# VectorE's 16-bit passes of far tiles are ordered behind GpSimd's norm steps in a conformer layer

## The chip, the cores and the metric

The kernel runs on 1 core of one Trainium2 chip. The metric is the device time of one execution in microseconds (us), the median of several runs. Five engines work side by side, each through its own queue in program order: PE (TensorE, matrix products), ACT (ScalarE, activation functions), DVE (VectorE, elementwise work), POOL (GpSimd) and SP (SyncE, which only issues DMAs here).

## The reference

Two sequences (B = 2) of T = 4000 tokens with D = 144 channels pass through one conformer layer; all tensors are bfloat16.

```python
h = _layernorm(x);  x = x + 0.5 * (_silu(h @ w_ff1a) @ w_ff1b)          # 144 -> 576 -> 144
h = _layernorm(x);  qkv = h @ w_qkv                                     # H = 4 heads of 36
p = _softmax(einsum('bhqd,bhkd->bhqk', q, k) * Dh ** -0.5)              # 4000 x 4000 per head
x = x + einsum('bhqk,bhkd->bhqd', p, v) @ w_o
h = _layernorm(x);  a, b = split(h @ w_pw1);  h = a * _sigmoid(b)
c = depthwise convolution of h over 5 tokens;  x = x + _silu(c) @ w_pw2
h = _layernorm(x);  x = x + 0.5 * (_silu(h @ w_ff2a) @ w_ff2b)
return _layernorm(x)
```

There are five layer norms per token, and 2 x 4 x 4000 x 4000 exponentials.

## The kernel before

Tokens are worked on in 16 chunks of up to 512 (8 per sequence). All of X stays in on-chip memory. The attention runs over 32 groups (a chunk of queries and a pair of heads), each over 31 tiles of 128 keys, with the last 32 keys apart (`rest`).

**A plan written by a scheduler.** The program has no fixed order. `Rec.op` (L55) records each instruction with its tiles and a cost in us, and keeps a clock of its own: `free[eng]` is the time at which an engine is done by the plan, `o.done` the time at which others may use the result. `Sched` holds the stages of all chunks as threads (Python generators). A thread asks for an engine with `need(eng, slots, kids, cond, rank)`; `slots` is something that has a time from which it is available (`best`). `start_of` works out when a thread could go on, `best` takes, among those within 0.05 us of the earliest, the one with the smallest rank, and `advance` lets it record its next instructions. When all is recorded, `finish` works out from the data dependences which semaphores each instruction must wait for, and `replay` writes each engine's queue in the recorded order. So every instruction has one line in the profile, L146. Costs decide the order; on the chip only data dependences hold anything back.

**Exponentials.** For most tiles PE writes scores to PS and ACT makes PT = exp(PS) of both heads of the pair at once (128 x 1024), `emit_exp`. To relieve ACT, DVE does some tiles by bit arithmetic. For a *far tile* (`far_tiles`, taken from the end of a group's list of tiles) DVE moves each head's scores into the 16-bit buffer PU (a `tensor_scalar` from PS, 128 x 512, cost 0.07 + 512/960). In a *split tile* DVE does so for one head and ACT does the other; two such halves share a PU buffer. There are NPD = 2 buffers of PU, PF and PC. `exact` (L965) then corrects the result in four passes over 128 x 1024 16-bit values, all from and to on-chip memory SBUF: PF <- PU (bitwise and, cost 0.335), PC <- PF (0.335), PC <- PC x PF (two inputs, 0.6), PU <- PU + PC (two inputs, 0.6). Then PE multiplies PU with VA, and the buffer is free. The passes have rank RELAX = 1, after everything else that could start at the same time, or HURRY = -2 where the group is nearly done.

**Norms.** `ln` works on half a chunk: DVE takes statistics (`bn_stats`, ST <- X), POOL makes 1/sqrt(var + eps) from them in two steps on 128 x 2 values (RS <- ST, cost 0.22; power, RS <- RS,NHALF, cost 0.71), and DVE applies it (XN, two instructions). Statistics and both POOL steps are recorded in one step of the thread. The result is turned by SP's transposing DMAs (by PE at the start and the end) and used by the next matrix product. POOL does nothing else in the main part but copies of convolution edges between chunks (UA <- UA, UB <- UB, in `post1`), for which the convolution on PE waits.

Of the kernel before, what the change touches and what calls it, by code (L numbers as in the profile page):

```python
# [28 lines left out]
LERP_B = 127.0 * 128.0 + 0.128  # L29
QUAD_C = 130.0  # L30
QUAD_K = 0.333 / 128.0


class Op:
# [3 lines left out]
class Rec:  # L38
# [8 lines left out]
    def __init__(self, nc):  # L47
        self.nc = nc
        self.ops = []
        self.n = {}  # L50
        self.hist = {}
        self.free = {e: 1.0 for e in self.ENGS}
        self.kind = None
        self.last = 0.0

    def op(self, eng, name, *a, r=(), w=(), q=None, cost=0.1, kind=None, lat=None, **k):
        o = Op()
        o.eng, o.name, o.a, o.k, o.q = eng, name, a, k, q
        o.deps, o.inc, o.cnt = [], False, 0
        lane = eng if q is None else "q:" + q  # L60
        o.idx = self.n.get(lane, 0)
        self.n[lane] = o.idx + 1
        for key in r:
            h = self.hist.setdefault(key, ([], []))
            o.deps += [(d, True) for d in h[0]]
            h[1].append(o)
        for key in w:
            h = self.hist.setdefault(key, ([], []))
            o.deps += [(d, False) for d in h[0] + h[1] if d is not o]
            if h[1] and not (len(h[1]) == 1 and h[1][0] is o):  # L70
                self.hist[key] = ([o], [])
            else:
                h[0].append(o)
        start = self.free[eng]
        for d, raw in o.deps:
            if d.eng != eng or d.q is not None or (raw and eng != "pe"):
                start = max(start, d.done - self.NEAR.get((d.eng, eng), 0.0))
        if eng == "pe":
            if kind != self.kind:
                start += 0.1  # L80
            self.kind = kind
        self.free[eng] = start + cost
        o.done = start + cost + (self.LAT[eng] if lat is None else lat) + (0.045 if kind == "q" else 0.0)
        self.last = o.done
        self.ops.append(o)
        return o

# [69 lines left out]
class Slots:  # L157
# [12 lines left out]
    def best(self):  # L170
        return min(self.free.values())

    def take(self):
        i = min(self.free, key=lambda j: (self.free[j], j))
        del self.free[i]
        self.held.add(i)
        return i
# [4 lines left out]
            self.free[i] = self.R.last  # L182


class Thread:
    def __init__(self, gen, ready):
        self.gen, self.ready, self.live = gen, ready, True
# [3 lines left out]
def need(eng, slots=None, kids=(), cond=None, rank=None):  # L191
    return (eng, slots, kids, cond, rank)
# [6 lines left out]
class Sched:  # L199
# [26 lines left out]
        return kids  # L226

    def advance(self, th, item):
        self.cur = th
        n0 = len(self.R.ops)  # L230
        self.stepped = False
        try:
            th.req = th.gen.send(item)
        except StopIteration:
            th.live = False
            self.threads.remove(th)
        new = self.R.ops[n0:]
        if new:
            th.ready = max(th.ready, max(o.done for o in new))
# [29 lines left out]
def bass_standalone__conformer_family_zipformer__speech_kernel(  # L269
# [27 lines left out]
    R = Rec(nc)  # L297
    op = R.op
    S = Sched(R)

    def sb(name, shape, dt=BF16):
        return nc.alloc_sbuf_tensor(name, [128] + list(shape), dt)
# [28 lines left out]
    PU = sb("PU", [NPD, 2, CH], U16)  # L331
    PF = sb("PF", [NPD, 2, CH], U16)
    PC = sb("PC", [NPD, 2, CH])
# [38 lines left out]
    def load(eng, q, dst, src, w, r=()):  # L372
        op(eng, "dma_start", dst, src, q=q, w=w, r=r, cost=0.7)
# [9 lines left out]
    def load_ff(eng, q, WA, WB, wa, wb, nm):  # L383
        load_k(eng, q, WA, wa, [(nm, "a", 0)], [nm + "0"])
        load(eng, q, WB[:, 0:4, :], wb[0:512, :].rearrange("(t p) d -> p t d", p=128), [(nm, "b", 0)])
        for j in range(2):
            load(eng, q, WB[64 * j:64 * j + 64, 4 + j, :], wb[512:FF, :], [(nm, "b", 1 + j)])

    op("dve", "memset", WA1[0:HD, 1, :], 0.0, w=["W10"], cost=0.7)
    op("dve", "memset", WQKV[0:HD, 1, :], 0.0, w=["WQKV0"], cost=0.5)  # L390
    op("pool", "memset", XN[:, :, :, D:DP], 0.0, w=["XNP"], cost=2.0)
    for W, nm in ((WO, "WO0"), (WP1, "WP10"), (WA2, "W20")):
# [37 lines left out]
    for i in range(NWARM):  # L430
        op("pe", "matmul", PSV[:, i % 8, 0:256], lhsT=DUM[:, 0:128], rhs=DUM[:, :], start=True, stop=True,
           r=["DUM"], w=[("ps", i % 8)], cost=0.15)
# [522 lines left out]
    def late(more=0):  # L955
# [3 lines left out]
            return True  # L959
        return o_grp[0] // 2 - len(post_done) > (LAG if g < 20 else LAG_END) + more  # L960

    pair = [None]
    split = {}

    def exact(u, n, gi):  # L965


        def rank():
            return HURRY if s_grp[0] > gi or len(left[gi]) <= NEAR_END else RELAX

        yield need("dve", rank=rank)
        op("dve", "tensor_scalar", PF[:, u, :, 0:n], PU[:, u, :, 0:n], 127, None, op0=ALU.bitwise_and,
           r=[("PU", u)], w=[("PF", u)], cost=0.335)
        yield need("dve", rank=rank)
        op("dve", "tensor_scalar", PC[:, u, :, 0:n], PF[:, u, :, 0:n], QUAD_C, QUAD_K, op0=ALU.subtract, op1=ALU.mult,
           r=[("PF", u)], w=[("PC", u)], cost=0.335)
        yield need("dve", rank=rank)
        op("dve", "tensor_tensor", PC[:, u, :, 0:n], PC[:, u, :, 0:n], PF[:, u, :, 0:n], op=ALU.mult,
           r=[("PC", u), ("PF", u)], w=[("PC", u)], cost=0.6)
        yield need("dve", rank=rank)  # L980
        op("dve", "tensor_tensor", PU[:, u, :, 0:n], PU[:, u, :, 0:n], PC[:, u, :, 0:n], op=ALU.add,
           r=[("PC", u), ("PU", u)], w=[("PU", u)], cost=0.6)

    def bits_outputs(gi, u, kts, done):

        b, qc, p = groups[gi]
        n = width(gi)
        yield from exact(u, n, gi)
        yield need("pe", cond=lambda: o_grp[0] == gi and begun_group(gi))
        outputs(gi, [[] if kt is None else [(VA[:, b, kt, 2 * p + hh, :], PU[:, u, hh, :].bitcast(BF16))]  # L990
                     for hh, kt in enumerate(kts)],
                [("PU", u), "VA1"] + [("VA", b * CPB + c) for c in sorted({kt // NB for kt in kts if kt is not None})])
        pdp.give(u)
        output_done(gi, done)
# [51 lines left out]
    def next_tile():  # L1046

        g = s_grp[0]
        while g < len(groups) and not left[g]:
            g += 1  # L1050
        return (g, left[g][0]) if g < len(groups) else None

    def s_start():

        gi, kt = next_tile()
        b, qc, p = groups[gi]
        kc = b * CPB + kt // NB
        if kc not in kv_done or b * CPB + qc not in kv_done:
            return None
        t = max(R.free["pe"], R.ready(("WKT", kc)), R.ready(("WQT", (b * CPB + qc) % NQS)))  # L1060
        return max(t, exps[len(tiles) - 2]) if len(tiles) >= 2 else t
# [81 lines left out]
    while len(ff1_done) < CPB or 0 not in kv_done:  # L1143
        t, th = S.best()
        S.run(th)
    banks.restrict([6, 7])
    while banks.held - banks.only:
        t, th = S.best()
        S.run(th)

    for r in range(4):
        op("pe", "matmul", PSV[:, 4 + r // 2, r % 2 * 256:r % 2 * 256 + 256], lhsT=DUM[:, 0:128], rhs=DUM[:, :],
           start=True, stop=True, skip_group_check=True, r=["DUM"], w=[("ps", 4 + r // 2)], cost=0.107, kind="f")
# [20 lines left out]
    while next_tile() is not None or n_e < len(tiles):  # L1174
        a = s_start() if next_tile() is not None else R.free["pe"]
# [4 lines left out]
        t, th = S.best()  # L1180
# [23 lines left out]
    while o_grp[0] < len(groups):  # L1204
        emit_pending(force=True)
        if o_grp[0] < len(groups):
            t, th = S.best()
# [7 lines left out]
    while S.threads:  # L1215
        t, th = S.best()
# [34 lines left out]
```

## Time and profile before

| | |
|---|---|
| median of 3 runs | 986.31 us (985.67 to 987.59) |
| the profiled execution | 988.83 us, its span 987.0 us |
| ACT: exponentials PT <- PS | 808.9 us in 883 instructions |
| DVE: evictions PU <- PS | 189.8 us in 284 instructions |
| DVE: the four kinds of pass | 58.8 + 58.8 + 96.0 + 96.1 us, 143 of each |
| POOL: norm steps | 40.7 + 115.3 us, 160 of each |

The span is from the first to the last instruction of the core. A group's line gives the engine, the operation, the tiles written and read, shapes, the count, busy time and mean ns, and after the last bar the idle time of the engine ahead of such instructions with what ended it. A line of the timeline gives start, duration, engine, operation, tiles, and in brackets the engine's idle time before it and what released it. Matrix products are pipelined and their ends modelled. On DVE and ACT the shown durations of neighbours overlap a little, so what an instruction takes of the engine is read from start to start.

### The profile page before, as it was taken

The numbers are of one execution on the slowest core, as the hardware profiler recorded it, in microseconds if no ns is written. First come the engines' busy times: TensorE is split into PE (matmuls) and PEld (weight loads), VectorE is DVE, ScalarE is ACT, GpSimd is POOL, SyncE is SP. The second block draws the span as 40 slices with busy tenths as digits, with TensorE's granted clock in tenths as the row PEclk, the third lists the DMA queues.
The fourth block names the chain that finished last, engine by engine and source line by source line (L and its number), as shares of the span: only waits on it lengthen the run. The fifth ranks groups of instructions, "written<-read, shape, count | busy, mean of one in ns | idle before, by whom it ended". The sixth has DMA issues, their size and how long they took to land.

```text
span 987.0 us, 25520 instructions
## 1 busy us (share of the span) xinstructions
PE 893.5 (91%) x10852; PEld 344.3 (35%) x10852; DVE 846.0 (86%) x1903; ACT 908.4 (92%) x1168; POOL 168.8 (17%) x395
## 2 busy tenths in 40 slices
PE   8999898999898999999999998998889888898989
PEld 6733233232232323333343333333223232233358
DVE  7767999989988999988898999887898988887874
ACT  5798999999998999999999999998999999989952
POOL 6420020101013120211112020201111111101112
PEclk9999999999999999999999999999999999999999
DMA  4000020101011020111100010110001010101000
GB/s 135 2 1 2 12 43 13 33 2 39 18 29 33 13 44 9 22 28 24 23 8 12 12 35 12 29 13 17 18 13 29 13 29 12 29 2 25 16 18 13
DMA packets 73281, 21.67 MB, mean 22 GB/s; under 512 B 70592, under 2 KB 73168, under 8 KB 73168
## 3 DMA queue, kind: packets, MB, share of 16 engines
q1 hardware_dynamic: 72128, 19.58, 10.1%
q8 instruction: 85, 1.39, 0.6%
q10 hardware_dynamic: 1040, 0.48, 0.2%
q14 instruction: 28, 0.23, 0.1%
HBM read 3.31 MB, written 2.30 MB: 6 GB/s over the span
## 4 chain that ended last, share of the span: by engine, by line
PE 40%; ACT 36%; DVE 19%; POOL 3%; issue 2%; DMA 0%; SPq 0%; ACTq 0%
PE PS L146 40%; ACT PT L146 30%; DVE PU L146 6%; ACT TH L146 4%; DVE PC L146 3%; POOL RS L146 2%; DVE XN L146 2%; DVE OTF L146 1%; DVE HT L146 1%; DVE ST L146 1%; DVE X L146 1%; DVE PF L146 1%; ACT HT L146 1%; ACT PR L146 0%; DVE CB L146 0%
## 5 line engine op out<-in xcount | busy, mean ns | idle before, releaser
L146 ACT ACTIVATE PT<-PS 128x1024 bf16<-128x1024 f32 (+2 forms) x883 | 808.9, 1008 | 22.9 <-PE PS L146 20.3
L146 PE MATMUL PS<-QT,KT 64*64 64x512 bf16 (+2 forms) x4032 | 417.9, 391 | 58.1 <-ACT PT L146 44.9
L146 PE MATMUL PS<-PT,VA 64*37 64x512 bf16 (+1 forms) x3400 | 340.3, 374 | 2.5 <-DVE OTF L146 1.5
L146 PEld LDWEIGHTS PS<-QT,KT 64*64 64x64 bf16 (+1 forms) x4032 | 122.6, 103 | 322.4 <-ACT PT L146 193.3
L146 DVE TENSOR_SCALAR PU<-PS 128x512 uint16<-128x512 f32 (+1 forms) x284 | 189.8, 674 | 26.1 <-PE PS L146 23.2
L146 POOL TENSOR_SCALAR RS<-ST 128x2 f32<-128x2 f32 (+1 forms) x160 | 40.7, 254 | 707.9 <-DVE ST L146 707.3
L146 POOL TENSOR_TENSOR RS<-RS,NHALF 128x2 f32<-128x2 f32 (+1 forms) x160 | 115.3, 720 | 13.4
L146 PEld LDWEIGHTS PS<-PT,VA 64*37 64x37 bf16 x3400 | 98.5, 96 | 18.4 <-DVE OTF L146 2.5
L146 DVE TENSOR_SCALAR XN<-X,ST,RS 128x144 bf16<-128x144 bf16 (+1 forms) x310 | 82.6, 313 | 17.5 <-POOL RS L146 16.7
L146 DVE TENSOR_TENSOR PC<-PC,PF 128x1024 bf16<-128x1024 bf16 (+1 forms) x143 | 96.0, 675 | 1.6
L146 DVE TENSOR_TENSOR PU<-PU,PC 128x1024 uint16<-128x1024 uint16 (+1 forms) x143 | 96.1, 673 | 1.2
L146 ACT ACTIVATE TH<-PS 128x512 bf16<-128x512 f32 (+2 forms) x140 | 84.5, 604 | 5.2 <-PE PS L146 4.2
L146 PE MATMUL PS<-XT,WA 72*128 72x512 bf16 (+3 forms) x256 | 71.8, 379 | 7.0 <-DVE PU L146 2.9
L146 DVE SCALAR_TENSOR_TENSOR X<-PS,X 128x288 bf16<-128x288 f32 (+1 forms) x128 | 56.6, 453 | 23.1 <-PE PS L146 22.0
L146 DVE SCALAR_TENSOR_TENSOR HT<-TH,PS 128x512 bf16<-128x512 bf16 (+2 forms) x110 | 67.7, 620 | 5.5 <-ACT TH L146 5.2
L146 DVE BATCH_NORM_STATS2 ST<-X 128x6 f32<-128x288 bf16 (+1 forms) x160 | 69.0, 451 | 0.7
L146 PE MATMUL PS<-PU,VA 64*37 64x512 bf16 (+1 forms) x568 | 55.9, 378 | 9.2 <-DVE PU L146 8.4
L146 DVE TENSOR_SCALAR PC<-PF 128x1024 bf16<-128x1024 uint16 (+1 forms) x143 | 58.8, 414 | 1.6
L146 DVE TENSOR_SCALAR PF<-PU 128x1024 uint16<-128x1024 uint16 (+1 forms) x143 | 58.8, 416 | 1.1
L146 PE MATMUL PS<-WB,HT 128*128 128x144 bf16 (+1 forms) x640 | 56.4, 228 | 2.1 <-DVE HT L146 1.2
L146 PEld LDWEIGHTS PS<-WB,HT 128*128 128x128 bf16 (+1 forms) x640 | 39.9, 101 | 36.1 <-issue 22.3
L146 DVE TENSOR_REDUCE OTF<-PS 128x512 f32<-128x1024 f32 (+1 forms) x32 | 38.4, 1200 | 16.1 <-PE PS L146 15.2
(97 smaller groups left out, 623.2 us busy)
## 6 DMA issues: line engine op xcount, KB each, us to landing
X<-in_x_dram SPq DMA_DIRECT2D x14, 144.0 KB, 3.7
out_dram<-XN SPq DMA_DIRECT2D x28, 72.0 KB, 1.8
XT<-XN SPq DMA_TRANSPOSE x82, 2.5
XT<-AN SPq DMA_TRANSPOSE x28, 2.5
X<-in_x_dram SPq DMA_DIRECT2D x2, 117.0 KB
out_dram<-XN SPq DMA_DIRECT2D x4, 58.5 KB
WA<-in_w_ff1a_dram ACTq DMA_DIRECT2D x1, 144.0 KB, 2.9
WB<-in_w_ff1b_dram ACTq DMA_DIRECT2D x1, 144.0 KB, 3.5
```

Of the source, the lines that this page charges most:

```text
L146: ins = getattr(eng, o.name)(*o.a, **o.k)
```

## The change

The plan's clock learns about two things. (1) An instruction marked `port=True`, which are the four passes of `exact`, is taken to hold off GpSimd: a POOL instruction that would end by the plan before the last such pass has ended is put at that pass's end + 0.13; and if a pass starts while the last POOL instruction is running by the plan and ends after it, that instruction's end, and the time at which its thread goes on, move to the pass's end + 0.13. (2) Each pass asks for a `Quiet` slot, available from POOL's planned end less SLACK = 0.6 us; until then the scheduler gives DVE to other threads, or plans a hole. No instruction gets a wait; the arithmetic is unchanged.

```diff
+SLACK = 0.6
...
-    def op(self, eng, name, *a, r=(), w=(), q=None, cost=0.1, kind=None, lat=None, **k):
+        self.run_end = 0.0
+        self.behind = None
+        self.cur = None
+
+    def op(self, eng, name, *a, r=(), w=(), q=None, cost=0.1, kind=None, lat=None, port=False, **k):
...
-        self.free[eng] = start + cost
-        o.done = start + cost + (self.LAT[eng] if lat is None else lat) + (0.045 if kind == "q" else 0.0)
+        end = start + cost
+        if eng == "pool" and self.run_end > end - 0.05:
+            end = self.run_end + 0.13
+        if port:
+            self.run_end = end
+            if self.behind is not None and start < self.free["pool"] - 0.05 < end:
+                p, th = self.behind
+                late = end + 0.13 - self.free["pool"]
+                self.free["pool"] += late
+                p.done += late
+                if th is not None:
+                    th.ready = max(th.ready, p.done)
+        self.free[eng] = end
+        o.done = end + (self.LAT[eng] if lat is None else lat) + (0.045 if kind == "q" else 0.0)
         self.last = o.done
+        if eng == "pool":
+            self.behind = (o, self.cur)
...
+class Quiet:
+    free = True
+
+    def __init__(self, R):
+        self.R = R
+
+    def best(self):
+        return self.R.free["pool"] - SLACK
+
+    def take(self):
+        return None
...
-        self.cur = th
+        self.cur = self.R.cur = th
...
+    quiet = Quiet(R)
...
-        yield need("dve", rank=rank)
+        yield need("dve", quiet, rank=rank)
         op("dve", "tensor_scalar", PF[:, u, :, 0:n], PU[:, u, :, 0:n], 127, None, op0=ALU.bitwise_and,
-           r=[("PU", u)], w=[("PF", u)], cost=0.335)
+           r=[("PU", u)], w=[("PF", u)], cost=0.335, port=True)
```

The other three passes of `exact` are changed in the same two places.

More of the change, by code (lines that the diff above doesn't have):

```diff
@@ L969, in rank @@
             return HURRY if s_grp[0] > gi or len(left[gi]) <= NEAR_END else RELAX
-        yield need("dve", rank=rank)
+        yield need("dve", quiet, rank=rank)
         op("dve", "tensor_scalar", PF[:, u, :, 0:n], PU[:, u, :, 0:n], 127, None, op0=ALU.bitwise_and,
-           r=[("PU", u)], w=[("PF", u)], cost=0.335)
-        yield need("dve", rank=rank)
+           r=[("PU", u)], w=[("PF", u)], cost=0.335, port=True)
+        yield need("dve", quiet, rank=rank)
         op("dve", "tensor_scalar", PC[:, u, :, 0:n], PF[:, u, :, 0:n], QUAD_C, QUAD_K, op0=ALU.subtract, op1=ALU.mult,
-           r=[("PF", u)], w=[("PC", u)], cost=0.335)
-        yield need("dve", rank=rank)
+           r=[("PF", u)], w=[("PC", u)], cost=0.335, port=True)
+        yield need("dve", quiet, rank=rank)
         op("dve", "tensor_tensor", PC[:, u, :, 0:n], PC[:, u, :, 0:n], PF[:, u, :, 0:n], op=ALU.mult,
-           r=[("PC", u), ("PF", u)], w=[("PC", u)], cost=0.6)
-        yield need("dve", rank=rank)
+           r=[("PC", u), ("PF", u)], w=[("PC", u)], cost=0.6, port=True)
+        yield need("dve", quiet, rank=rank)
         op("dve", "tensor_tensor", PU[:, u, :, 0:n], PU[:, u, :, 0:n], PC[:, u, :, 0:n], op=ALU.add,
-           r=[("PC", u), ("PU", u)], w=[("PU", u)], cost=0.6)
+           r=[("PC", u), ("PU", u)], w=[("PU", u)], cost=0.6, port=True)
     def bits_outputs(gi, u, kts, done):
```

## The prediction

> **What bounds the kernel now.** I read the page first: the busy shares, the chain that ended last, the costliest groups.
>
> ```profile
> span 987.0 us, 25520 instructions
> PE 893.5 (91%) x10852; PEld 344.3 (35%) x10852; DVE 846.0 (86%) x1903; ACT 908.4 (92%) x1168; POOL 168.8 (17%) x395
> PE 40%; ACT 36%; DVE 19%; POOL 3%; issue 2%; DMA 0%; SPq 0%; ACTq 0%
> L146 ACT ACTIVATE PT<-PS 128x1024 bf16<-128x1024 f32 (+2 forms) x883 | 808.9, 1008 | 22.9 <-PE PS L146 20.3
> L146 POOL TENSOR_SCALAR RS<-ST 128x2 f32<-128x2 f32 (+1 forms) x160 | 40.7, 254 | 707.9 <-DVE ST L146 707.3
> L146 POOL TENSOR_TENSOR RS<-RS,NHALF 128x2 f32<-128x2 f32 (+1 forms) x160 | 115.3, 720 | 13.4
> L146 DVE TENSOR_TENSOR PC<-PC,PF 128x1024 bf16<-128x1024 bf16 (+1 forms) x143 | 96.0, 675 | 1.6
> ```
>
> PE and ACT share the end; DVE and POOL matter where they make those two late. ACT spends 808.9 of its 908.4 us on the attention exponentials. An order is better if it leaves ACT fewer gaps or moves more exponentials to DVE.
>
> Then the part in which far tiles run, in the windows view: 62 to 945 us as a whole, and of the eight 100 us stretches from 100 to 900 the first, the emptiest and the last.
>
> ```profile
> 62.00:945.00 883.00, 797.66 (x9747) 275.13 (x9744) 775.33 (x1681) 849.75 (x1061) 126.36 (x290) 0.99 0.11 20
> 100.00:200.00 100.00, 89.12 (x1104) 29.80 (x1104) 95.30 (x201) 98.41 (x119) 11.78 (x28) 1.00 0.14 25
> 300.00:400.00 100.00, 90.06 (x1050) 30.43 (x1050) 89.80 (x197) 93.60 (x117) 19.51 (x43) 0.98 0.15 27
> 800.00:900.00 100.00, 86.35 (x1065) 28.19 (x1068) 88.16 (x183) 94.73 (x115) 13.90 (x30) 0.98 0.10 18
> ```
>
> The columns are PE, weight loads, DVE, ACT, POOL. ACT is busy 849.75 of 883 us, so it idles 33; DVE idles 108. Between stretches ACT's idle time goes from 1.6 to 6.4 us, a standard deviation of about 1.6.
>
> Then GpSimd's two norm steps by tile (shortest, middle, longest ns), and, from the waits of 62 to 945 us, who waits for them and what ACT waits for.
>
> ```profile
> L146 POOL TENSOR_SCALAR RS<-ST x160: 188/193/1492, 5.6 to 981.6; 128x2 f32<-128x2 f32 x140, 104x2 f32<-104x2 f32 x20
> L146 POOL TENSOR_TENSOR RS<-RS,NHALF x160: 690/690/1138, 5.9 to 981.9; 128x2 f32<-128x2 f32 x140, 104x2 f32<-104x2 f32 x20
> ```
>
> ```profile
> DVE XN L146 <- POOL RS L146: 8.8, 13, 1.1
> ```
>
> ```profile
> ACT PT L146 <- PE PS L146: 20.3, 45, 3.1
> ```
>
> So most norm steps run unhindered, and a few are held off, one to 1.49 us. Against 160 steps at the middle duration the surplus is 40.7 − 160 × 0.193 = 9.8 us and 115.3 − 160 × 0.69 = 4.9 us. That is the whole resource that the change is about: some 15 us on an engine with 17% load. What counts is how much of it reaches ACT.
>
> Last, the timeline at the two kinds of place where it does. First a copy of convolution edges on GpSimd:
>
> ```profile
> 310.54 0.69 DVE L146 TENSOR_TENSOR PC<-PC,PF 128x1024 bf16<-128x1024 bf16 x1
> 310.69 2.13 POOL L146 COPY UA<-UA 128x2 bf16<-128x2 bf16 x1 [1.85 <-DVE UA L146]
> 311.14 0.43 DVE L146 TENSOR_SCALAR PC<-PF 128x1024 bf16<-128x1024 uint16 x1
> 311.48 0.69 DVE L146 TENSOR_TENSOR PU<-PU,PC 128x1024 uint16<-128x1024 uint16 x1
> 312.08 0.69 DVE L146 TENSOR_TENSOR PC<-PC,PF 128x1024 bf16<-128x1024 bf16 x1
> ...
> 313.00 1.04 PE L146 MATMUL PS<-UA,DG 128*128 128x512 bf16 x3 [2.62 <-POOL UB L146]
> ...
> 314.66 1.02 ACT L146 ACTIVATE PT<-PS 128x1024 bf16<-128x1024 f32 x1 [3.12 <-PE PS L146]
> ...
> 316.65 0.60 ACT L146 ACTIVATE TH<-PS 128x512 bf16<-128x512 f32 x1 [0.97 <-PE PS L146]
> ```
>
> The copy lasts until the row of four passes is over; PE stands 2.62 us in front of the convolution, and ACT idles 3.12 + 0.97 us behind it. Then a norm step:
>
> ```profile
> 830.88 0.45 DVE L146 BATCH_NORM_STATS2 ST<-X 128x6 f32<-128x288 bf16 x1
> ...
> 831.25 0.67 DVE L146 TENSOR_TENSOR PC<-PC,PF 128x1024 bf16<-128x1024 bf16 x1
> ...
> 831.42 1.49 POOL L146 TENSOR_SCALAR RS<-ST 128x2 f32<-128x2 f32 x1 [1.12 <-DVE ST L146]
> ...
> 831.84 0.42 DVE L146 TENSOR_SCALAR PF<-PU 128x1024 uint16<-128x1024 uint16 x1
> ...
> 832.18 0.68 DVE L146 TENSOR_TENSOR PU<-PU,PC 128x1024 uint16<-128x1024 uint16 x1
> ...
> 832.99 0.69 POOL L146 TENSOR_TENSOR RS<-RS,NHALF 128x2 f32<-128x2 f32 x1
> ...
> 833.72 0.55 DVE L146 TENSOR_SCALAR XN<-X,ST,RS 128x144 bf16<-128x144 bf16 x2 [0.86 <-POOL RS L146]
> ...
> 836.58 0.40 PE L146 MATMUL PS<-PU,VA 64*37 64x512 bf16 x4 [1.04 <-DVE PU L146]
> ...
> 837.25 1.94 ACT L146 ACTIVATE PT<-PS 128x1024 bf16<-128x1024 f32 x2 [0.56 <-PE PS L146]
> ```
>
> DVE loses 0.86 us, PE 1.04, ACT 0.56. The same place in three other rounds of the loop:
>
> ```profile
> 724.88 1.02 ACT L146 ACTIVATE PT<-PS 128x1024 bf16<-128x1024 f32 x1 [0.43 <-PE PS L146]
> ```
>
> ```profile
> 782.09 1.02 ACT L146 ACTIVATE PT<-PS 128x1024 bf16<-128x1024 f32 x1 [0.56 <-PE PS L146]
> ```
>
> ```profile
> 893.89 1.02 ACT L146 ACTIVATE PT<-PS 128x1024 bf16<-128x1024 f32 x1 [0.63 <-PE PS L146]
> ```
>
> **The change part by part.** No instruction, wait or DMA is added or removed as such. The change alters the plan's clock, and with it the order in the queues and the choice of far and split tiles.
>
> *What can be won.* The ACT gaps behind held-off GpSimd are 3.12 + 0.97 + 0.43 + 0.56 + 0.56 + 0.63 = 6.27 us. The other 8.8 − 4 × 0.86 = 5.4 us of norm waits on DVE lead to no ACT gap that I can find; I count them as zero. Their cover is DVE's 108 us of idle time; without it they would be worth at most those 5.4 us.
>
> *How much of it is won.* The queue of DVE gets no wait. A held-off step is eased only if the plan finds another DVE instruction to put ahead of the passes; if it finds none, it leaves a hole in its own clock, the order stays, and the chip runs the passes at once as before. From the code's costs, POOL's planned end lies 0.146 + 0.22 + 0.08 + 0.71 = 1.16 us after a norm's statistics (on the chip, 0.17 to the start and 0.19 + 0.69 of work give about as much). Less SLACK that closes DVE to passes for 0.56 us. DVE runs 1681 instructions in 883 us, of which 4 × 143 are passes: 1109 others, one per 0.80 us, so 0.56/0.80 = 0.7 of one per closed window. They come in runs, so I take half of the windows as having a substitute: 6.27/2 = **3.1 us gained**.
>
> *What it may cost.* A pass that is put off keeps its PU buffer (there are two) longer, so the next far tile starts later, and tiles that DVE doesn't take fall to ACT. Worst case: 116 norm steps of 62 to 945 us × 0.56 = 65 us of DVE lost. A far tile takes DVE 2 × 0.60 (evictions, by the code's cost) + 2 × 0.34 + 2 × 0.60 (passes, start to start above) = 3.1 us, so 65 us are 21 tiles of 0.92 us on ACT: +19 us. Best case: nothing lost, since the closed window is filled by work that had to be done anyway, and DVE looking free draws in a few split tiles, each 0.5 us off ACT. I take 0: DVE idles 108 us already, and nearest to the row is that the hole exists in the plan alone. Both ends stay in the range.
>
> *What the model over-counts.* The change treats all four kinds of pass alike. Two neighbouring cases:
>
> ```profile
> 136.05 0.69 POOL L146 TENSOR_TENSOR RS<-RS,NHALF 128x2 f32<-128x2 f32 x1
> 136.20 0.68 DVE L146 TENSOR_TENSOR PU<-PU,PC 128x1024 uint16<-128x1024 uint16 x1
> ```
>
> ```profile
> 188.63 1.14 POOL L146 TENSOR_TENSOR RS<-RS,NHALF 128x2 f32<-128x2 f32 x1
> ...
> 189.13 0.42 DVE L146 TENSOR_SCALAR PF<-PU 128x1024 uint16<-128x1024 uint16 x1
> ```
>
> The pass with two inputs (136.20) covers the end of the power step, which stays at 0.69; the pass with one input (189.13) stretches it to 1.14. At 831.42 the two-input pass did hold a step that was starting. The Trainium skill says the same, "SBUF — State Buffer", section "Who interferes with whom": a VectorE instruction with two SBUF inputs contends with a GpSimd one that reads SBUF, not with one that only writes. By that rule half of the holding-back is needless, which would take something off the gain. I add no term for it: the plan then believes RS to be late by up to 0.13 + 0.60 us and queues XN behind other work, and such a delay is covered as the 5.4 us above are.
>
> *Sum.* The profiled execution took 988.83 us (span 987.0), 2.5 above the median of the runs, 986.31. −3.1 gives 985.7 for it and **983.2 us** for the median. A new order also redraws ACT's gaps: eight stretches with a deviation of 1.6 give 1.6 × √8 = 4.6 us either way, more than the effect itself.
>
> **The rivals.**
>
> *Slower: passes put off lose far tiles.* Place: the two PU buffers, between a norm's statistics and 0.56 us later. For it: DVE is at 95.30 of 100 us in the first stretch, and PE already waits for PU. Against: DVE idles 108 us overall. It decides once 3.1 us of ACT, 3.4 tiles, 10.5 us of DVE are lost, that is 0.09 us per norm step. At half the worst case: 986.3 − 3.1 + 9.6 = 992.8 us.
>
> *The order doesn't do what it says.* The closed windows find nothing to fill them, or the chip's clock drifts against the plan, and as many steps are held off as before, elsewhere. For it: no wait enforces the order; at 831.25 only passes stood between the statistics and XN. Time: 986.3 us.
>
> *All of it is won.* Every window has a substitute, and PE's clock doesn't dip (0.98 in the stretch of the 310 us case): 986.3 − 6.3 = 980.0 us.
>
> **How the numbers follow.** About 0.2% (2 us) is what a measurement of this kernel can tell from no change. Forecast 0.45, slower rival 0.28, no effect 0.14, all won 0.13. With the scatter, the forecast gives faster/same/slower 0.29/0.13/0.03, the slower rival 0.02/0.03/0.23, no effect 0.04/0.06/0.04, all won 0.13/0/0: 0.48, 0.22, 0.30. The likeliest case's own range is 983.2 ± 4.6, 978.6 to 987.8. For 8 in 10 the range reaches down to 980.0 − 4.6, about 975, and up a little past the slower rival, to 994.
>
> **What would show it.** Right: the longest norm step falls well below 1.49 us, the 2.13 us copy is gone, the surplus falls from 15 to about 7 us, DVE's waits for RS fall below 8.8, exponentials on ACT stay within 3 of 883, ACT's idle time falls by 3 us. The slower rival: fewer than 143 sets of passes and more ACT exponentials. No effect: rows of passes directly behind norm statistics, with steps of over 1 us. The forecast is wrong in kind if the time moves by over 5 us while the surplus on POOL stays, since that is then only a redrawn order.

## The result and the profile after

The changed kernel takes 978.56 us (977.23 to 980.43, 6 runs), beside it before 986.52 us (985.67 to 988.10, 6 runs). The ratio is 0.9918, with a 95% interval of 0.9904 to 0.9933: 0.8% faster. The forecast was 983.2 us, the range 975 to 994.

The page of the changed kernel (its lines are L164 where before has L146): span, busy time, chain, and three of the groups that the prediction showed.

```profile
span 978.6 us, 25427 instructions
PE 889.3 (91%) x10816; PEld 340.9 (35%) x10816; DVE 841.2 (86%) x1892; ACT 908.3 (93%) x1164; POOL 162.5 (17%) x395
ACT 48%; PE 38%; DVE 11%; DMA 1%; issue 1%; POOL 1%; ACTq 0%
...
L164 ACT ACTIVATE PT<-PS 128x1024 bf16<-128x1024 f32 (+2 forms) x878 | 812.5, 1030 | 17.7 <-PE PS L164 14.3
...
L164 POOL TENSOR_SCALAR RS<-ST 128x2 f32<-128x2 f32 (+1 forms) x160 | 31.1, 194 | 707.5 <-DVE ST L164 707.3
L164 POOL TENSOR_TENSOR RS<-RS,NHALF 128x2 f32<-128x2 f32 (+1 forms) x160 | 117.6, 735 | 13.3
```

DVE and POOL have gone from 22% of the chain to 12%, ACT from 36% to 48%. The surplus of the norm steps over their usual duration is 31.1 − 160 × 0.191 = 0.5 us and 117.6 − 160 × 0.689 = 7.4 us, 7.9 in all against 14.7 before. It has left the first step and grown in the second, as the durations (shortest, middle, longest ns) say:

```profile
L164 POOL TENSOR_SCALAR RS<-ST x160: 184/191/288, 5.6 to 973.2; 128x2 f32<-128x2 f32 x140, 104x2 f32<-104x2 f32 x20
L164 POOL TENSOR_TENSOR RS<-RS,NHALF x160: 688/689/1530, 5.9 to 973.5; 128x2 f32<-128x2 f32 x140, 104x2 f32<-104x2 f32 x20
```

DVE's waits for RS, from 62 to 945 us, have fallen from 8.8 us:

```profile
DVE XN L164 <- POOL RS L164: 2.1, 7, 0.4
```

What the new order looks like, from the timeline at the longest step (start, duration):

```profile
475.92 0.45 DVE L164 BATCH_NORM_STATS2 ST<-X 128x6 f32<-128x288 bf16 x1
...
476.29 0.57 DVE L164 TENSOR_SCALAR PU<-PS 128x416 uint16<-128x416 f32 x1
476.46 0.19 POOL L164 TENSOR_SCALAR RS<-ST 128x2 f32<-128x2 f32 x1 [1.86 <-DVE ST L164]
...
476.73 1.53 POOL L164 TENSOR_TENSOR RS<-RS,NHALF 128x2 f32<-128x2 f32 x1
476.78 0.65 DVE L164 TENSOR_SCALAR PF<-PU 128x832 uint16<-128x832 uint16 x2
...
477.35 0.37 DVE L164 TENSOR_SCALAR PC<-PF 128x832 bf16<-128x832 uint16 x1
...
477.67 0.69 DVE L164 SCALAR_TENSOR_TENSOR HT<-TH,PS 128x512 bf16<-128x512 bf16 x1
...
478.30 0.55 DVE L164 TENSOR_SCALAR XN<-X,ST,RS 128x144 bf16<-128x144 bf16 x2
```

An eviction now stands between the statistics and the passes, and the first step isn't held (0.19 us); the passes come 0.6 us before the second step should end and hold it to 1.53 us; but HT follows them, not XN, and DVE doesn't wait. Between 62 and 945 us, 26 of 116 statistics had a pass directly behind them in DVE's queue before, and 6 of 116 have one now.

In sum: from the first to the last exponential, ACT's gaps fall from 33.7 to 27.4 us and its work from 864.7 to 862.1; what follows the last exponential goes from 37.9 to 38.4 us. So far this reads like the forecast, only larger. The experiments say otherwise about the cause.

### The profile page after: what moved, and what is told of

Read it like the earlier page. It is cut to its first block, busy times and chain, and to the rows that moved or that the text cites. A ratio compares the mean times of both kernels' runs of the same rounds, so it can differ in the third digit from the quotient of the medians.

```text
span 978.6 us, 25427 instructions
## 1 busy us (share of the span) xinstructions
PE 889.3 (91%) x10816; PEld 340.9 (35%) x10816; DVE 841.2 (86%) x1892; ACT 908.3 (93%) x1164; POOL 162.5 (17%) x395
## 4 chain that ended last, share of the span: by engine, by line
ACT 48%; PE 38%; DVE 11%; DMA 1%; issue 1%; POOL 1%; ACTq 0%
ACT PT L164 41%; PE PS L164 38%; ACT TH L164 4%; DVE PU L164 3%; DVE PC L164 2%; DVE OTF L164 1%; DVE HT L164 1%; DMA XT<-XN 1%; POOL RS L164 1%; DVE XN L164 1%; ACT HT L164 1%; DVE PF L164 1%; ACT PR L164 1%; DVE X L164 0%; DMA XT<-AN 0%
## 5 line engine op out<-in xcount | busy, mean ns | idle before, releaser
L164 ACT ACTIVATE PT<-PS 128x1024 bf16<-128x1024 f32 (+2 forms) x878 | 812.5, 1030 | 17.7 <-PE PS L164 14.3
L164 PE MATMUL PS<-QT,KT 64*64 64x512 bf16 (+2 forms) x4032 | 422.7, 390 | 62.2 <-ACT PT L164 51.8
L164 PE MATMUL PS<-PT,VA 64*37 64x512 bf16 (+1 forms) x3404 | 336.8, 373 | 2.4 <-DVE OTF L164 1.5
L164 PEld LDWEIGHTS PS<-QT,KT 64*64 64x64 bf16 (+1 forms) x4032 | 123.4, 103 | 339.2 <-ACT PT L164 225.7
L164 DVE TENSOR_SCALAR PU<-PS 128x512 uint16<-128x512 f32 (+1 forms) x282 | 189.0, 673 | 23.7 <-PE PS L164 20.9
L164 POOL TENSOR_SCALAR RS<-ST 128x2 f32<-128x2 f32 (+1 forms) x160 | 31.1, 194 | 707.5 <-DVE ST L164 707.3
L164 POOL TENSOR_TENSOR RS<-RS,NHALF 128x2 f32<-128x2 f32 (+1 forms) x160 | 117.6, 735 | 13.3
L164 PEld LDWEIGHTS PS<-PT,VA 64*37 64x37 bf16 x3404 | 96.7, 96 | 16.4 <-DVE OTF L164 2.2
L164 DVE TENSOR_TENSOR PC<-PC,PF 128x1024 bf16<-128x1024 bf16 (+1 forms) x141 | 94.8, 674 | 1.6
L164 DVE TENSOR_TENSOR PU<-PU,PC 128x1024 uint16<-128x1024 uint16 (+1 forms) x141 | 94.6, 672 | 1.0
L164 ACT ACTIVATE TH<-PS 128x512 bf16<-128x512 f32 (+3 forms) x140 | 89.1, 638 | 5.5 <-PE PS L164 4.7
L164 DVE TENSOR_SCALAR XN<-X,ST,RS 128x144 bf16<-128x144 bf16 (+1 forms) x310 | 82.7, 311 | 11.1 <-POOL RS L164 9.9
L164 DVE SCALAR_TENSOR_TENSOR X<-PS,X 128x288 bf16<-128x288 f32 (+1 forms) x128 | 56.4, 452 | 30.4 <-PE PS L164 29.5
L164 PE MATMUL PS<-XT,WA 72*128 72x512 bf16 (+3 forms) x256 | 71.1, 378 | 4.2 <-DVE HT L164 1.7
L164 DVE SCALAR_TENSOR_TENSOR HT<-TH,PS 128x512 bf16<-128x512 bf16 (+3 forms) x110 | 67.4, 619 | 8.3 <-ACT TH L164 7.7
L164 DVE BATCH_NORM_STATS2 ST<-X 128x6 f32<-128x288 bf16 (+1 forms) x160 | 69.0, 450 | 0.7
L164 DVE TENSOR_SCALAR PC<-PF 128x1024 bf16<-128x1024 uint16 (+1 forms) x141 | 58.0, 414 | 1.9
L164 PE MATMUL PS<-PU,VA 64*37 64x512 bf16 (+1 forms) x564 | 56.2, 377 | 3.7 <-DVE PU L164 3.3
L164 DVE TENSOR_SCALAR PF<-PU 128x1024 uint16<-128x1024 uint16 (+1 forms) x141 | 57.8, 415 | 1.2
L164 PE MATMUL PS<-WB,HT 128*128 128x144 bf16 (+1 forms) x640 | 56.8, 228 | 1.2 <-ACT HT L164 0.9
L164 PEld LDWEIGHTS PS<-WB,HT 128*128 128x128 bf16 (+1 forms) x640 | 40.2, 102 | 32.7 <-issue 21.1
L164 DVE TENSOR_REDUCE OTF<-PS 128x512 f32<-128x1024 f32 (+1 forms) x32 | 38.4, 1199 | 13.4 <-PE PS L164 13.3
```

What stands on the lines that cost most here:

```text
L164: ins = getattr(eng, o.name)(*o.a, **o.k)
```

## The experiments

All times are medians of runs beside before on the same chip (986.5 to 987.0 us); ratios to before have their 95% interval in brackets.

**1 and 2. Both orders without their waits for GpSimd.** In the main part XN takes its scale from a constant tile, and the convolution reads zero edges, so both leave a part of the computation out; the plan reckons with the true dependences, so the order of every queue is that of before (of the changed kernel), apart from seven small fills at the start.

```diff
-               RS[0:tb, u, i, 0:1], ..., r=[("X", c, 2 * g + i), ("ST", u), ("RS", u)],
+               RSC[0:tb, i, 0:1] if main else RS[0:tb, u, i, 0:1], ...,
+               r=[("X", c, 2 * g + i), ("ST", u), ("RS", u), "RSC"], plan=[("RS", u)] if main else (),
...
-            (UA[:, us, 2:4, 0:1], UA[:, up, 2:4, TB:TB + 1], ...      # edge copies, likewise the others
+            (UXA[:, 0, us, :, :], UA[:, up, 2:4, TB:TB + 1], ...
...
-               r=[("U", us), ("UL", us), ("UR", us), "DG"]             # convolution
+               r=[("U", us), ("UL", us), ("UR", us), "DG", "UZ"], plan=[("UL", us), ("UR", us)]
```

Before's order: 

> The order of before in every queue, but nothing in the main part waits for GpSimd: XN is scaled by a constant instead of RS, and the convolution reads zero edges instead of GpSimd's copies (both left out of the computation; GpSimd still does its steps). Hold-off theory (the gain is waiting for held-off GpSimd that went away): this order without the waits comes near the changed kernel, 978 to 980.5 us. Redraw theory (the new order is better for reasons that have nothing to do with GpSimd): the 6.27 us of ACT gaps behind held-off steps go at most in part, 982 to 986 us.

The changed order: 

> The order of the changed kernel, with the same waits left out in the same way (constant scale, zero edges). Hold-off theory: little is left to win, 977 to 978.5 us, and the distance to the same treatment of before's order is under 2 us. Redraw theory: 976 to 978.5 us, and the distance between the two orders stays at 5 to 8 us.

Measured: 976.48 us, ratio 0.9905 [0.9889, 0.9921], and 974.86 us, 0.9883 [0.9865, 0.9901], both a little below either theory's figures; the first theory's pattern, near each other and far from before, is what came out. Waits for GpSimd cost before's order 9.4 us (by the ratio; 10.5 by the medians) and the changed order 0.9918 − 0.9883, or 3.5 us. Without them the two orders are 1.6 us apart, with overlapping intervals. So in this pair of orders, most of the 8 us, some 5.9, is waiting for GpSimd that went away. Where it was, the trace of before's order without the waits shows, here at the edge copy that held up the convolution (before: 310.69 to 316.65):

```profile
310.21 0.61 PE L147 MATMUL PS<-UA,DG 128*128 128x512 bf16 x3
310.53 2.12 POOL L147 COPY UXA<-UA 128x2 bf16<-128x2 bf16 x1 [1.80 <-DVE UA L147]
...
312.68 0.60 ACT L147 ACTIVATE TH<-PS 128x512 bf16<-128x512 f32 x1 [0.34 <-PE PS L147]
```

The copy takes its 2.12 us as ever, but PE is no longer behind it, and ACT's TH starts at 312.68 instead of 316.65. Set beside each other, the start of each ACT instruction in the two traces gives the price of each place, as the growth of the distance between the two: 3.86 us here, 0.64, 0.83, 0.83 and 0.84 at the four norm steps quoted in the prediction, 1.6 and 1.5 at 684 to 689 and 876 to 881 us, where before's PE ran at half clock (last section), about 1.2 after the last exponential, the rest in pieces under 0.7. Together these are 12.8 us, the distance of the two traces (987.0 and 974.2 us); the medians are 10.5 apart, since the profiled execution lay above the median in before (988.83 against 986.98) and below it in the other (975.97 against 976.48).

**3 and 4. Each half of the change alone.** In one, passes aren't kept back (shown for one of the four; the others likewise):

```diff
-        yield need("dve", quiet, rank=rank)
+        yield need("dve", rank=rank)
```

> The plan's clock reckons with GpSimd held off by the passes, but the passes aren't kept back (no Quiet slot). Hold-off theory by keeping passes back: most of the gain is missing, 983 to 987 us, and norm steps of over 1 us stay in the TENSOR_SCALAR of RS. If it is the plan's knowledge of the late RS that helps (XN queued later, other work in its place): 978 to 981 us with the surplus on GpSimd as large as before. Redraw theory: anything from 977 to 991 us.

In the other, they are kept back, but the plan's clock knows of no hold-off (again one of four):

```diff
-           r=[("PU", u)], w=[("PF", u)], cost=0.335, port=True)
+           r=[("PU", u)], w=[("PF", u)], cost=0.335)
```

> Passes are kept back until 0.6 us before GpSimd's planned end, but the plan knows of no hold-off. Hold-off theory by keeping passes back: most of the gain, 978 to 981 us, and the first norm step at 0.19 us throughout. If the plan's knowledge helps: 984 to 987 us. Redraw theory: anything from 977 to 991 us.

Measured: 979.73 us, 0.9946 [0.9926, 0.9965], and 979.24 us, 0.9930 [0.9914, 0.9947]. Each half alone brings most of the whole, 0.54% and 0.70% of 0.82%. With the plan's knowledge alone, time and surplus (15.8 us) are as the second theory has them, but not for its reason: norm steps of 1.83 and 2.40 us occur, DVE still waits 6.4 us for RS (8.8 before), and PE still stands 2.61 us in front of the convolution at 313 us, the place that was dearest in before. With the passes kept back alone the surplus falls to 6.3 us, but the first step still reaches 1.49 us and DVE waits 6.6 us for RS. Two halves that each give most of the whole, one of them with GpSimd held off as before, are what one would see if any new order did. That called for orders that are new for no reason.

**5 to 8. Orders redrawn by a hair.** Three costs that have nothing to do with GpSimd are moved a little, each in before:

```diff
-               ... w=[("XT", s, g)], cost=1.2, lat=2.0)      # null1: a transposing DMA
+               ... w=[("XT", s, g)], cost=1.2, lat=2.05)
...
-           cost=0.24)                                        # null2: the reciprocal
+           cost=0.25)
...
-        return 0.05 + n / 1200.0                              # null3: every ScalarE instruction
+        return 0.053 + n / 1200.0
```

and the third also in the changed kernel (null6).

> Before, with one cost of the plan moved by a hair that has nothing to do with GpSimd: the transposing DMA's landing at 2.05 instead of 2.0 us. The order is redrawn (2394 lines of VectorE's queue differ), the hold-off stays unknown to the plan. Hold-off theory: near before, 984 to 989 us, with norm steps of over 1 us. Redraw theory: such a redraw reaches the changed kernel's time as easily, 977 to 983 us.

> As null1, but VectorE's reciprocal is reckoned at 0.25 instead of 0.24 us. Hold-off theory: 984 to 989 us. Redraw theory: 977 to 983 us.

> As null1, but every ScalarE instruction is reckoned 0.003 us longer. Hold-off theory: 984 to 989 us. Redraw theory: 977 to 983 us.

> The changed kernel with the same hair as null3 (every ScalarE instruction 0.003 us longer in the plan). Hold-off theory: the gain holds in a redrawn order, 976 to 981 us, no norm wait of over 0.5 us on VectorE. Redraw theory: it scatters over the same range as the redrawn orders of before.

Measured: 970.49 us, 0.9842 [0.9822, 0.9862]; 977.69 us, 0.9909 [0.9895, 0.9924]; 972.26 us, 0.9853 [0.9838, 0.9868]; and null6 974.39 us, 0.9873 [0.9857, 0.9890]. All three redrawn orders of before beat it by as much as the change does or by more, and null1 beats the changed kernel by 8 us. Only null2 falls into a range that a theory gave; null1 and null3 are faster than either had it. null6 gains too, though DVE's norm waits reach 0.7 us in it. GpSimd is held off in null1 at least as much as in before, as its page, its norm steps and its waits from 62 to 945 us show:

```profile
span 968.0 us, 25402 instructions
PE 885.2 (91%) x10801; PEld 341.5 (35%) x10801; DVE 839.5 (87%) x1896; ACT 905.5 (94%) x1159; POOL 169.7 (18%) x395
...
L146 POOL TENSOR_TENSOR RS<-RS,NHALF 128x2 f32<-128x2 f32 (+1 forms) x160 | 120.4, 753 | 13.4
```

```profile
L146 POOL TENSOR_SCALAR RS<-ST 128x2 f32<-128x2 f32 (+1 forms) x160 | 38.7, 242 | 683.8 <-DVE ST L146 683.8
```

```profile
L146 POOL TENSOR_SCALAR RS<-ST x160: 188/193/1492, 5.6 to 962.6; 128x2 f32<-128x2 f32 x140, 104x2 f32<-104x2 f32 x20
```

```profile
DVE XN L146 <- POOL RS L146: 8.3, 15, 1.1
```

Its surplus is 38.7 − 30.9 + 120.4 − 110.4 = 17.8 us against 14.7 in before, its longest first step the same 1.49 us, its waits on DVE 8.3 against 8.8 us, and it is 16 us faster. It lacks before's dearest place, since its longest edge copy takes 0.69 us, not 2.13; that is only a part of the 16 us, as 9 and 10 show. What GpSimd loses says little about the time; where it loses it says more. The hold-off theory, as a theory of why the changed order is better than before, holds for this pair; as a statement about the change it needs the other pairs.

**9 and 10. What the waits cost the redrawn orders.** null1 and null2 with their waits for GpSimd left out as in 1.

> The order of null1 (970.49 us) without the waits for GpSimd, as in b_nopool (constant norm scale and zero convolution edges, so these parts of the computation are left out). Unlucky-order theory (before's order happened to put held-off steps where PE and ACT wait for them, and most redrawn orders don't, though GpSimd is held off as much): 967 to 969.5 us, a gain of 1 to 3.5 us against 10.5 in before's order. Rival (GpSimd costs every order without the change's knowledge about the same, and null1 is faster for other reasons): 960 to 963 us.

> The same for null2 (977.69 us), in which the convolution waits once 2.6 us for a held-off edge copy, as in before. Unlucky-order theory: the waits of this order are dearer than those of null1 and cheaper than before's, 4 to 8 us, 970 to 974 us. Rival: 967 to 968 us, like before's 10.5.

Measured: 965.55 us, 0.9792 [0.9775, 0.9808], and 969.11 us, 0.9829 [0.9811, 0.9846]. By the ratios the waits cost null1 4.9 us and null2 7.9, against before's 9.4 and the changed order's 3.5. Both times fall between the two expectations: no order gets off free, and before's is the dearest of three, though its distance to null2 is within the intervals. But the orders also differ without any such wait: 965.6, 969.1, 974.9 (changed) and 976.5 us (before).

**11 and 12. The changed kernel with the hairs of null1 and null2.**

> The changed kernel with the hair of null1 (transposing DMA at 2.05 us), its pair. Unlucky-order theory: the change has no fixed worth, so this comes out anywhere in 968 to 982 us and may well be slower than null1's 970.49. Rival (the knowledge is worth several us in any order): 963 to 968 us, faster than null1.

> The changed kernel with the hair of null2 (reciprocal at 0.25 us), its pair. This hair moves only 571 lines of VectorE's queue against the changed kernel. Unlucky-order theory: near the changed kernel, 976 to 981 us, not below null2's 977.69 by more than 2 us. Rival (the knowledge is worth several us in any order): 969 to 974 us.

Measured: 975.61 us, 0.9897 [0.9879, 0.9915], and 980.62 us, 0.9941 [0.9924, 0.9958]. Both are slower than their partners. The four pairs, as ratios to before:

| hair | without the change | with it | difference |
|---|---|---|---|
| none | 1 | 0.9918 | −0.0082 |
| transposing DMA | 0.9842 | 0.9897 | +0.0055 |
| reciprocal | 0.9909 | 0.9941 | +0.0032 |
| ScalarE costs | 0.9853 | 0.9873 | +0.0020 |
| mean | 0.9901 | 0.9907 | +0.0006 |

Over the pairs the change is worth nothing that four pairs can show: the differences have a standard deviation of 0.0061, so their mean has a standard error of 0.003, and with four pairs a gain or loss of up to 1% stays possible. Only the first pair shows a gain, and it was in before's order that the costly places had been found. (The orders aren't all independent: null5's differs from the changed kernel's by only 571 lines of DVE's queue.) Orders without it scatter by 0.0072 (7.1 us), orders with it by 0.0029; with four of each this hints at a narrower scatter and doesn't prove one.

Yet the change does to the order what it is meant to do in all four. Between 62 and 945 us, 26, 39, 38 and 35 norm statistics have a pass directly behind them without it (in the order of the table), and 6, 8, 6 and 5 with it; DVE's waits for RS go from 8.8, 8.3, 9.4 and 4.9 us to 2.1, 4.5, 2.9 and 7.0. The times don't follow.

Long holds remain with the change, as null4 shows in the timeline of its longest step:

```profile
423.46 0.53 DVE L164 TENSOR_SCALAR XN<-X,ST,RS 128x144 bf16<-128x144 bf16 x2
423.63 0.19 POOL L164 TENSOR_SCALAR RS<-ST 128x2 f32<-128x2 f32 x1 [0.38 <-DVE ST L164]
423.90 4.38 POOL L164 TENSOR_TENSOR RS<-RS,NHALF 128x2 f32<-128x2 f32 x1
423.90 0.75 DVE L164 TENSOR_SCALAR PF<-PU 128x1024 uint16<-128x1024 uint16 x2
424.57 0.75 DVE L164 TENSOR_SCALAR PC<-PF 128x1024 bf16<-128x1024 uint16 x2
425.24 1.28 DVE L164 TENSOR_TENSOR PC<-PC,PF 128x1024 bf16<-128x1024 bf16 x2
426.45 1.28 DVE L164 TENSOR_TENSOR PU<-PU,PC 128x1024 uint16<-128x1024 uint16 x2
```

The passes of both PU buffers come together, eight in a row, and start with the power step, which lasts 4.38 us, to 0.55 us after the row. Keeping passes back might gather such rows, but that isn't shown: null1, which keeps nothing back, has the same row at 451.96 us.

```profile
451.96 0.74 DVE L146 TENSOR_SCALAR PF<-PU 128x1024 uint16<-128x1024 uint16 x2
452.05 4.28 POOL L146 TENSOR_TENSOR RS<-RS,NHALF 104x2 f32<-104x2 f32 x1
```

## Why the prediction was right, step by step

- *Direction and range* were right: 978.56 us is inside 975 to 994, and faster had the largest chance, 0.48. The gain was 8 us instead of 3.1. The mechanism was right for this pair of orders, where most of the gain is waits that went away. That before was an order in which these waits stood in dear places was luck: in the other three pairs the changed kernel is the slower one, in one of them within the intervals.
- *What can be won, 6.27 us,* was too small. The same places cost 3.86 + 0.64 + 0.83 + 0.83 + 0.84 = 7.0 us in the comparison of the two traces of before's order, the half-clock stretches some 3.1 more, and all waits together 9.4 by the ratio. Counting ACT's gaps at the places was near for them and left out the rest.
- *Half of the windows find a substitute* was somewhat low: statistics with a pass directly behind them fell from 26 to 6, the waits' cost from 9.4 to 3.5 us, by 63%. With that share the 6.27 us would have given 3.9.
- *Lost far tiles, taken as nothing,* was right. ACT's exponentials by shape, before and after:

```profile
L146 ACT ACTIVATE PT<-PS 128x1024 bf16<-128x1024 f32 x714 | 691.7, 1058 | 17.0 <-PE PS L146 14.6
...
L146 ACT ACTIVATE PT<-PS 128x512 bf16<-128x512 f32 x58 | 37.8, 651 | 3.6 <-PE PS L146 3.6
```

```profile
L164 ACT ACTIVATE PT<-PS 128x1024 bf16<-128x1024 f32 x721 | 701.4, 1075 | 13.2 <-PE PS L164 10.3
...
L164 ACT ACTIVATE PT<-PS 128x512 bf16<-128x512 f32 x46 | 29.5, 644 | 3.3 <-PE PS L164 3.3
```

  In full tiles that is 714 + 29 = 743 and 721 + 23 = 744: one more on ACT, not the 10 of the slower rival. DVE made 141 sets of passes instead of 143.
- *The signs named* came in part: the surplus fell to 7.9 us, DVE's waits for RS to 2.1, and no edge copy takes more than 0.76. Two failed: the longest norm step is 1.53 us, not well below 1.49 (it is a second step now), and ACT has 878 exponential instructions, 5 fewer than before and not within 3, though the work is the same within a tile.
- *The redrawn order, 4.6 us either way,* is the step that was used wrongly, and perhaps sized too small: four orders of before scatter by 7.1 us, which four draws don't clearly tell from 4.6. I let the scatter work around before's own time, as if before were a typical draw; its three redrawn orders are 9 to 16 us faster. A kernel whose time hangs on one written-out order has to be placed among its neighbours first.
- *The test for "wrong in kind"* (a move of over 5 us while the surplus on POOL stays) was passed, since the surplus halved. It was no test: null1 moves by 16 us with a larger surplus, and the changed kernel could have fallen by 8 us through any redrawing. What would have told was the pairs.
- *The rival that the order doesn't do what it says* is false as to the order, in all four pairs (6, 8, 6 and 5 statistics with a pass behind them), and partly true as to the hold (steps of 1.53 us here, 4.38 in null4, 2.50 in null6).

What stays open: whether the change narrows the scatter of orders, and what makes null1's order 9 to 11 us better than before's and the changed one's even without any wait for GpSimd (965.6 against 976.5 and 974.9 us). The traces without waits of null1's and before's orders say where the distance lies, not why: ACT's work from the first to the last exponential is 5.1 us less (858.2 against 863.3), of which 3.0 are the same exponentials done in 873 instead of 883 instructions with fewer halves of split tiles; its gaps are 3.4 us less (20.0 against 23.4), and what follows the last exponential 1.6 us less. The part of the two-input passes was not tried by itself.

## What to carry to other kernels

Where a scheduler writes the order of the queues, a change of a cost can redraw most of it, and the redraw may be worth more than the change: move two or three unrelated costs by a hair, with and without the change, and compare the means, before believing in a mechanism. To price a wait in a given order, keep the order and take away only what is waited for; the starts of the same instructions in the two traces then give the cost place by place. The fastest kernel of this study is before with one DMA reckoned at 2.05 us, 1.6% faster than before and no better founded than any other draw.

## What the runs showed of the hardware

PE's granted clock was halved for three stretches of 3.41 us in before, and each followed a stretch of the same length in which PE was busy for 0.81, 1.89 and 2.09 us, so 24% to 61% by the profile. The windows view, each stretch ahead and the stretch itself (PE is the first engine column; the clock stands behind POOL's):

```profile
309.39:312.80 3.41, 0.81 (x10) 0.13 (x8) 3.38 (x8) 2.14 (x3) 2.11 (x2) 1.00 0.44 90
681.49:684.90 3.41, 1.89 (x26) 0.66 (x26) 2.66 (x6) 3.22 (x4) 1.25 (x2) 1.00 0.09 22
872.59:876.00 3.41, 2.09 (x30) 0.54 (x25) 3.01 (x5) 3.27 (x5) 0.00 (x0) 1.00 0.00 0
```

```profile
312.80:316.20 3.40, 3.20 (x20) 0.92 (x21) 0.69 (x1) 1.02 (x1) 0.14 (x2) 0.50 0.02 5
684.90:688.30 3.40, 3.40 (x32) 1.50 (x26) 0.69 (x1) 1.62 (x2) 0.00 (x0) 0.50 0.09 22
876.00:879.40 3.40, 3.40 (x26) 1.16 (x26) 2.33 (x7) 2.06 (x3) 0.00 (x0) 0.50 0.02 5
```

The Trainium skill, "TensorE: Matmul & The Clock Gate", section "What's actually happening", puts the half clock behind an idle window of about 3.4 us; the length agrees, but here windows that were 55% and 61% busy were enough. The busy share doesn't settle it: the window from 101.20 us is 55% busy too, starts a whole number of times 3.413 us (61, 170 and 226) ahead of the three, and the full clock follows it.

```profile
101.20:104.61 3.41, 1.88 (x32) 0.61 (x28) 3.38 (x9) 2.66 (x4) 0.00 (x0) 1.00 0.38 77
104.61:108.02 3.41, 2.76 (x40) 0.89 (x36) 3.31 (x7) 3.36 (x5) 0.00 (x0) 1.00 0.02 5
```

So a stall of PE can be paid a second time: at the two later stretches ACT lost 1.6 and 1.5 us against before's order without waits for GpSimd, which had no such stretch (its mean clock is 1.000, before's 0.995). The scatter of before's runs goes with it: in the runs beside the experiments, the two with a mean clock of 1.000 took 983.51 and 984.39 us, those with 0.998 took 984.5 to 985.9, with 0.997 986.4 to 987.6, and with 0.995 987.65 to 988.3.

The two-input passes leave the end of a power step alone, as the prediction read from one pair of rows: in before, the 13 steps over whose usual end a two-input pass ran, with no one-input pass in them, took 0.69 us each, and the 6 over whose usual end a one-input pass ran took 0.84 to 1.14. But once a one-input pass holds the step, the two-input passes behind it hold it too (null4's 4.38 us, past the end of the row of eight).
